# A list-scheduled attention and gating kernel: corrected operation times, new ranks, and fillers of the first gap counted at the lower clock

## Chip, cores, metric

One core of one Trainium2 chip. The metric is device time in microseconds of one execution, from runs without a profile; the profile comes from one more execution. The core has five engines with a queue of instructions each: TensorE (PE, matmuls into PSUM), VectorE (DVE), ScalarE (ACT), GpSimd (POOL) and SyncE (SP), which here issues all DMAs.

## What is computed

Attention over 4 batches, 8 heads, 768 positions and a head dimension of 64, with 8 global columns and a causal band of 96, then a gated layer with a spatial mixing step. Cut to what matters:

```
scores = q @ k.T / sqrt(D) - slope[h] * dist      # kept where global or within the band
a = softmax(scores);  x = a @ v                   # heads side by side: (4, 768, 512)
h = relu(x @ w_in);  u, v = halves of h
v_n = layernorm(v)
v_s = w_spatial @ v_n + b_spatial
out = (u * v_s) @ w_out
```

`w_in` and `w_out` arrive as float64.

## The kernel before

The work goes in 24 blocks of 128 positions, six to a batch. A block has scores (token S, four pairs of heads, two halves), the softmax, the transposes of the probabilities and their products with the values (token A), and behind it the gated layer of the batch in pieces: V and U (products with the two halves of `w_in`), G (spatial mixing) and O (product with `w_out`). From block 6 on each operand of a matmul is split into a high and a low part (names with `h` and `l` at the end) and three products are added up. The six blocks of batch 0 use plain fp32 matmuls, two passes each in the trace, because then the other engines are still setting up: bias tables, the pieces of `w_in` (token I, eight pieces of 128x512) and `w_out` (Q, eight of 128x256), rebuilt from float64 bits, and the spatial weights (T, six of 128x768).

A piece of weights is rebuilt in `split_weights`: ACT takes the absolute value of the upper words into a staging buffer (`raw` or `rawh`), a clamp between two limits follows (a tensor-scalar with max and min, on DVE or POOL as the planner chooses), then on DVE a shift-and-mask and two shift-ors with the words in `u` or `pth`, then a rounding into the high part (`w_in_h`, `w_out_h`) and a subtraction for the low part (`w_in_l`, `w_out_l`). For the spatial weights (`setup_w_t`) there is a rounding into `w_t_h` and a subtraction into `w_t_l`, which is always POOL's.

No order is written out by hand. A recorder collects all operations, with the engines that each may run on (`either`). `plan` simulates five engines: an operation becomes ready when those it depends on have ended by its estimate, each engine takes the ready operation with the lowest rank, and of several engines the one that would finish it first. An operation's rank is its token's number in the table `KEYS`. The estimates are in `cost`: nanoseconds as a constant plus a term in n, the elements of a row. Its third value says that the operation uses the port that DVE and POOL share; two such operations don't overlap in the plan. `keep_warm` then goes through the planned order and fills gaps of PE of over 0.9 us in the plan, up to 150 us, with fillers: transposes of the identity into a PSUM bank that is free. The first gap begins at `WARM_FROM`, 3000 ns. The operations are issued in the planned order; on the chip every engine keeps its order and waits on semaphores, whatever the real durations are.

All instructions of this path have line 39 in the profile, where the recorder calls the engine; they are told apart by their tiles. `pr` are probabilities, `mn` the minima that a score pass on DVE (CUSTOM_DVE_ANT_0, in the order ISA) also gives, `p`, `s`, `ops`, `m` PSUM banks for transposes, scores, attention outputs and the gated layer, `c` sums of attention outputs, `xth` and `xtl` their parts.

Of the kernel before, what the change touches and what calls it, by code (L numbers as in the profile page):

```python
# [194 lines left out]
def cost(op):  # L195

    out = op.writes[0]
    n = elements(out)
    src = op.reads[0] if op.reads else out
    psum = any(in_psum(x) for x in op.reads + op.writes[:1])  # L200
    parts = list(out.ap)[0][1]
    if op.eng == "tensor":
        if op.call == "transpose":
            return 109, 0, False
        n = elements(op.kw["rhs"])
        if op.kw["rhs"].dtype == F32:
# [78 lines left out]
def plan(ops, keys, trace=None):  # L285
# [145 lines left out]
WARM_FROM, WARM_GAP, WARM_TO = 3000.0, 900.0, 150000.0  # L431
# [3 lines left out]
def attn_then_spatial_gating_kernel(  # L435
# [712 lines left out]
```

## Time and profile before

| | |
|---|---|
| median of 3 runs | 483.08 us (482.77 to 485.05) |
| profiled execution, its own time | 483.04 us |
| its span, first to last instruction | 480.8 us |
| mean granted TensorE clock | 0.998 |
| busy: PE, DVE, ACT, POOL | 463.2, 351.8, 273.9, 267.1 us |

Busy times are of the 480.8 us. A matmul's end is modelled and overlaps the next, so PE's busy time is no measure of its work; distances from start to start are. A row gives a group of instructions with its engine, output, inputs, count, busy time, mean and the idle time before them, with what ended it ("<-").

### The profile page before, as it was taken

The numbers are of one execution on the slowest core, as the hardware profiler recorded it, in microseconds if no ns is written. First come the engines' busy times: TensorE is split into PE (matmuls) and PEld (weight loads), VectorE is DVE, ScalarE is ACT, GpSimd is POOL, SyncE is SP. The second block draws the span as 40 slices with busy tenths as digits, with TensorE's granted clock in tenths as the row PEclk, the third lists the DMA queues.
The fourth block names the chain that finished last, engine by engine and source line by source line (L and its number), as shares of the span: only waits on it lengthen the run. The fifth ranks groups of instructions, "written<-read, shape, count | busy, mean of one in ns | idle before, by whom it ended". The sixth has DMA issues, their size and how long they took to land.

```text
span 480.8 us, 9763 instructions
## 1 busy us (share of the span) xinstructions
PE 463.2 (96%) x3186; PEld 424.5 (88%) x3186; DVE 351.8 (73%) x1017; ACT 273.9 (57%) x764; POOL 267.1 (56%) x388
## 2 busy tenths in 40 slices
PE   7888999999999999999999999999999999999996
PEld 7666779999899999989998988999999989999995
DVE  4999998865788978878776687885679577653232
ACT  4855984544567777776354486774386366521111
POOL 4165675466756888798581456888268233551000
PEclk9999999999999999999999999999999999999999
DMA  7944512746578777657554727755386250000111
GB/s 226 328 133 139 183 49 74 199 121 164 135 190 218 193 190 192 169 156 180 149 141 123 201 84 197 188 152 125 73 219 171 65 144 35 0 1 3 44 45 50
DMA packets 35915, 65.47 MB, mean 136 GB/s; under 512 B 6065, under 2 KB 6321, under 8 KB 35857
## 3 DMA queue, kind: packets, MB, share of 16 engines
q1 hardware_dynamic: 35856, 64.77, 49.0%
q8 instruction: 27, 0.44, 0.4%
q14 instruction: 32, 0.25, 0.2%
HBM read 29.76 MB, written 6.68 MB: 76 GB/s over the span
## 4 chain that ended last, share of the span: by engine, by line
PE 77%; DVE 12%; DMA 4%; ACT 2%; SPq 2%; issue 1%; POOL 1%; DVEq 0%; ACTq 0%; POOLq 0%
PE m L39 55%; PE ops L39 8%; PE s L39 7%; PE p L39 7%; DVE raw L39 3%; DVE pr L39 2%; DVE c L39 2%; SPq L39 2%; DVE rawh L39 1%; DMA u<-in_moe_w_in_dram 1%; DMA vring<-in_moe_w_spatial_dram 1%; ACT pr L39 1%; DVE ev L39 1%; DVE w_in_l L39 1%; DMA kring<-raw 1%
## 5 line engine op out<-in xcount | busy, mean ns | idle before, releaser
L39 ACT ACTIVATE pr<-pr,mn 128x256 f32<-128x256 f32 (+1 forms) x192 | 92.0, 482 | 21.5 <-DVE mn L39 21.0
L39 DVE CUSTOM_DVE_ANT_0 pr<-s,bias 128x256 f32<-128x256 f32 (+1 forms) x192 | 68.3, 396 | 16.9 <-PE s L39 14.6
L39 DVE TENSOR_TENSOR c<-ops,c 64x256 f32<-64x256 f32 x168 | 70.6, 420 | 9.1 <-ACT c L39 4.4
L39 POOL TENSOR_SCALAR pr<-pr,rc 128x256 f32<-128x256 f32 (+1 forms) x144 | 66.9, 484 | 16.4 <-DVE rc L39 9.2
L39 PE MATMUL ops<-pth,vring 128*128 128x256 f32 x352 | 70.3, 313 | 2.5 <-ACT pth L39 1.8
L39 PE MATMUL s<-kring,q 128*128 128x256 f32 (+1 forms) x384 | 68.4, 303 | 3.3 <-DVE mn L39 2.1
L39 ACT ACTIVATE pth<-p 128x512 fp32r<-128x512 f32 (+3 forms) x96 | 52.3, 557 | 29.8 <-PE ops L39 15.3
L39 PEld LDWEIGHTS s<-kring,q 128*128 128x128 f32 x384 | 56.6, 189 | 9.0 <-DVE mn L39 3.7
L39 PEld LDWEIGHTS ops<-pth,vring 128*128 128x128 f32 x352 | 54.3, 189 | 8.1 <-ACT pth L39 3.1
L39 PE MATMUL p<-ident,pr 128*128 128x128 f32 x352 | 56.3, 273 | 1.7 <-ACT c L39 1.3
L39 DVE TENSOR_TENSOR pth<-p,pth 128x512 fp32r<-128x512 f32 (+1 forms) x72 | 45.4, 642 | 10.3 <-ACT pth L39 9.4
L39 PEld LDWEIGHTS p<-ident,pr 128*128 128x128 f32 x352 | 42.1, 140 | 8.1 <-ACT c L39 2.4
L39 PE MATMUL m<-w_t_h,vnh 128*128 128x256 f32 x288 | 44.8, 284 | 0.0
L39 PE MATMUL m<-w_t_h,vnl 128*128 128x256 f32 x288 | 44.7, 284 | 0.0
L39 PE MATMUL m<-w_t_l,vnh 128*128 128x256 f32 x288 | 43.1, 281 | 0.0
L39 DVE TENSOR_TENSOR ev<-m,b_bc 128x512 f32<-128x512 f32 x24 | 16.5, 688 | 36.3 <-PE m L39 36.3
L39 POOL TENSOR_TENSOR vnl<-ev,vnh 128x512 fp32r<-128x512 f32 x24 | 31.2, 1302 | 18.5 <-DVE vnh L39 9.3
L39 ACT ACTIVATE gh<-ev 128x512 fp32r<-128x512 f32 x24 | 15.1, 630 | 45.6 <-DVE ev L39 45.5
L39 ACT ACTIVATE ev<-m 128x512 f32<-128x512 f32 (+1 forms) x36 | 21.3, 591 | 34.0 <-PE m L39 33.3
L39 PEld LDWEIGHTS m<-w_t_h,vnh 128*128 128x128 f32 x288 | 38.5, 189 | 0.7 <-DVE ev L39 0.3
L39 PEld LDWEIGHTS m<-w_t_h,vnl 128*128 128x128 f32 x288 | 38.6, 189 | 0.2
L39 POOL TENSOR_TENSOR xtl<-c,xth 128x256 fp32r<-128x256 f32 x40 | 30.9, 773 | 13.9 <-ACT xth L39 13.7
(139 smaller groups left out, 1004.8 us busy)
## 6 DMA issues: line engine op xcount, KB each, us to landing
q<-rawh SPq DMA_DIRECT2D x72, 128.0 KB, 2.4
q<-raw SPq DMA_DIRECT2D x72, 128.0 KB, 2.4
out_dram<-ev SPq DMA_DIRECT2D x23, 256.0 KB, 2.8
raw<-in_q_dram SPq DMA_DIRECT2D x18, 256.0 KB, 3.0
raw<-in_v_dram SPq DMA_DIRECT2D x18, 256.0 KB, 2.9
raw<-in_k_dram SPq DMA_DIRECT2D x18, 256.0 KB, 3.3
kring<-rawh SPq DMA_DIRECT2D x36, 128.0 KB, 2.4
kring<-raw SPq DMA_DIRECT2D x36, 128.0 KB, 2.4
```

The costliest lines, as they stand in the source:

```text
L39: getattr(self.real, self.call)(*self.args, **self.kw)
```

## The change

Three edits. In `cost`, the estimates of some operations are replaced: among others POOL's clamps (until now 155 + 0.84 n) get 210 + 3.34 n, POOL's two-input operations and its products with a column get a little more, and several of DVE's and ACT's. In `keep_warm`, fillers of the first gap are counted with 185 ns each and no longer 112. And the table of ranks is another one: nearly all of its numbers are different.

```diff
         if in_psum(src):
-            return (175 + .85 * n, 0, False) if parts < P else (66 + .83 * n, 0, False)
+            return (175 + .85 * n, 0, False) if parts < P else (70 + .86 * n, 0, False)
         return 112 + .83 * n, 0, False
     if op.eng == "gpsimd":
         if n <= 8:
             t = 600 if op.kw.get("op") == ALU.pow else 280
         elif op.call == "tensor_tensor":
-            t = 148 + 2.17 * n
+            t = 148 + 2.21 * n
+        elif op.kw.get("op0") == ALU.max:
+            t = 210 + 3.34 * n
         elif isinstance(op.kw.get("scalar1"), bass.AP):
-            t = 244 + .82 * n
+            t = 270 + .9 * n
...
     if op.call == "reciprocal":
-        return 70 + 6.25 * n, 85, False
+        return 90 + 6.25 * n, 85, False
...
     if op.call in ("tensor_reduce", "bn_stats"):
-        return 70 + 1.04 * elements(src), 0, False
+        return 120 + 1.06 * elements(src), 0, False
     if op.call == "bn_aggr":
-        return 99, 0, False
-    return (190 if parts < P else 74) + 1.04 * n, 0, not one
+        return 145, 0, False
+    return (180 if parts < P else 66) + (1.04 if parts < P else 1.1) * n, 0, not one
...
                 if best and best[0] < last:
-                    out.extend(make(best[1]) for _ in range(int((gap - 300) // 112)))
+                    out.extend(make(best[1]) for _ in range(int((gap - 300) // (112 if last > WARM_FROM else 185))))
...
-KEYS = {'start': -11.92, ('P', 0): -8.84, ('bias', 0): -3.64, ('S', 0, 0): 19.47,
+KEYS = {'start': -18.36, ('P', 0): -14.95, ('bias', 0): 12.66, ('S', 0, 0): -4.23,
...
```

What it moves, at three places. First PE's and SP's beginning. PE's first rows are the fillers and the scores of block 0 (`kring` keys, `q` queries); of the difference:

```order
-L39 MATMUL s_103<-ident 128x128 x36
+L39 MATMUL s_103<-ident 128x128 x17
 L39 MATMUL s_103<-kring_97,q_0_95 128x128 x2
 L39 MATMUL s_106<-kring_97,q_0_95 128x128 x2
```

SP's first DMAs, before:

```order
L39 DMA vring_114<-in_v_dram 128x512
L39 DMA nraw<-in_n_global_dram 128x2
L39 DMA nraw<-in_n_local_dram 128x2
L39 DMA q_0_95<-in_q_dram 64x512 x2
L39 DMA kring_97<-in_k_dram 128x512
```

and now:

```order
L39 DMA nraw<-in_n_global_dram 128x2
L39 DMA nraw<-in_n_local_dram 128x2
L39 DMA q_0_95<-in_q_dram 64x512 x2
L39 DMA kring_97<-in_k_dram 128x512
L39 DMA q_0_96<-in_q_dram 64x512 x2
L39 DMA kring_97<-in_k_dram 128x512
L39 DMA u_119<-in_moe_w_in_dram 128x1024
L39 DMA vring_114<-in_moe_w_spatial_dram 128x768
L39 DMA kring_97<-in_k_dram 128x512
L39 DMA vring_114<-in_v_dram 128x512 x3
L39 DMA q_0_95<-in_q_dram 64x512 x2
L39 DMA u_115<-in_moe_w_in_dram 128x1024
```

There are 19 fillers fewer at the start, and the first load of values has gone from the head of SP's queue to behind the third block of keys. Further down PE gets fillers in four places (8, 5, 5 and 6) where two groups of 5 stood.

Second, POOL's queue behind the bias tables, before:

```order
L39 TENSOR_SCALAR kring_97<-kg 128x4x32
L39 TENSOR_SCALAR rawh_0_118<-rawh_0_118 128x512
L39 TENSOR_SCALAR xth_122<-c_1_129 128x2x128
L39 TENSOR_SCALAR w_t_h<-vring_114 128x768
L39 TENSOR_TENSOR w_t_l<-vring_114,w_t_h 128x768
L39 TENSOR_SCALAR xth_122<-c_2_134 128x2x128
L39 TENSOR_SCALAR kring_97<-kg 128x4x32
L39 TENSOR_TENSOR w_t_l<-vring_114,w_t_h 128x768
L39 TENSOR_TENSOR xtl_123<-c_2_134,xth_122 128x2x128
L39 TENSOR_SCALAR raw_113<-rc_102 128x512
L39 TENSOR_SCALAR rawh_0_121<-rawh_0_121 128x512
```

and now:

```order
L39 TENSOR_SCALAR w_t_h<-vring_114 128x768
L39 TENSOR_TENSOR w_t_l<-vring_114,w_t_h 128x768
L39 TENSOR_SCALAR kring_97<-kg 128x4x32
L39 TENSOR_SCALAR w_in_h<-raw_0_120 128x512
L39 TENSOR_SCALAR w_t_h<-vring_114 128x768
L39 TENSOR_TENSOR w_t_l<-vring_114,w_t_h 128x768
L39 TENSOR_SCALAR kring_97<-kg 128x4x32
L39 TENSOR_TENSOR xtl_123<-c_2_134,xth_122 128x2x128
L39 TENSOR_SCALAR w_t_h<-vring_114 128x768
L39 TENSOR_TENSOR w_t_l<-vring_114,w_t_h 128x768
L39 TENSOR_SCALAR raw_113<-rc_102 128x512
```

The clamps (`rawh` from `rawh`) are gone, here two of six in all, and the roundings into `xth`; roundings into `w_in_h` have come. Later two subtractions into `w_out_l` come too. DVE has the six clamps now.

Third, DVE where it rebuilds a piece of `w_in` (`raw` with `u`) and one of `w_out` (`raw` with `pth`), before:

```order
L39 SCALAR_TENSOR_TENSOR raw_0_120<-u_115,raw_0_120 128x512
L39 TENSOR_REDUCE rc_102<-sums_91 128x8
L39 SCALAR_TENSOR_TENSOR raw_0_116<-pth_125,raw_0_116 128x256
L39 SCALAR_TENSOR_TENSOR raw_0_120<-u_115,raw_0_120 128x512
L39 TENSOR_TENSOR c_1_129<-ops_93,c_0_128 64x256 x2
```

and now:

```order
L39 SCALAR_TENSOR_TENSOR raw_0_120<-u_115,raw_0_120 128x512
L39 SCALAR_TENSOR_TENSOR raw_0_116<-pth_125,raw_0_116 128x256
L39 TENSOR_TENSOR c_1_129<-ops_93,c_0_128 64x256 x2
L39 BN_STATS st_144<-ev_99 128x6
L39 COPY c_2_134<-p_126 128x256
L39 ISA pr_132,mn_101<-s_106,bias 128x256
L39 ISA mn_101 128x1
L39 TENSOR_TENSOR c_0_128<-ops_94,c_2_134 64x256 x2
L39 SCALAR_TENSOR_TENSOR raw_0_120<-u_115,raw_0_120 128x512
```

Between the two shift-ors of the same piece there were a reduction and another shift-or; now there are eight operations, six of which read PSUM.

## Rows read from the trace of the kernel before

**Rows 1.** Stages of the span: length, then each engine's busy us (count), clock, DMA.

```profile
0.00:12.00 12.00, 8.79 (x55) 8.60 (x55) 5.53 (x38) 4.97 (x19) 4.97 (x17) 1.00 0.71 226
12.00:72.00 60.00, 52.92 (x276) 42.15 (x274) 58.85 (x177) 46.47 (x143) 32.89 (x30) 1.00 0.51 167
72.00:476.00 404.00, 401.34 (x2860) 373.77 (x2858) 287.44 (x805) 222.04 (x604) 229.28 (x342) 1.00 0.49 129
476.00:480.80 4.80, 0.19 (x2) 0.00 (x0) 0.00 (x0) 0.39 (x1) 0.00 (x0) 0.84 0.36 121
```

**Rows 2.** Waits of PE after 76 us: who for whom, us in total, times, longest.

```profile
PE s L39 <- DVE mn L39: 0.7, 1, 0.7
PE ops L39 <- DVE pth L39: 0.6, 1, 0.6
PE m L39 <- ACT gh L39: 0.5, 1, 0.5
PE s L39 <- DMA kring<-raw: 0.5, 1, 0.5
PE p L39 <- DVE pth L39: 0.3, 1, 0.3
```

**Rows 3.** PE from 12 us: groups to 72 us, then two lines of time.

```profile
L39 PE MATMUL s<-kring,q 128*128 128x256 f32 x80 | 20.7, 387 | 2.0 <-DVE mn L39 1.2 <-issue 0.7
L39 PE MATMUL ops<-pth,vring 128*128 128x256 f32 x68 | 17.7, 385 | 1.8 <-ACT pth L39 1.8
L39 PE MATMUL p<-ident,pr 128*128 128x128 f32 x72 | 11.4, 276 | 1.5 <-ACT c L39 1.3 <-ACT pth L39 0.2
...
12.07 1.99 PE L39 MATMUL s<-kring,q 128*128 128x256 f32 x8
13.90 0.27 PE L39 MATMUL p<-ident,pr 128*128 128x128 f32 x1
```

**Rows 4.** The first 13 us in order of time: start, us, engine, what, idle before.

```profile
0.72 0.39 SPq L39 DMA_DIRECT2D vring<-in_v_dram  x1
...
1.17 0.42 SPq L39 DMA_DIRECT2D nraw<-in_n_global_dram  x1
...
3.05 6.65 PE L39 MATMUL s<-ident 128*128 128x128 f32 x36 [3.05 <-POOL ident masks.py:199]
...
7.10 0.37 POOL L39 TENSOR_SCALAR kg<-kring 128x128 f32<-128x128 f32 x1 [3.25 <-DMA kring<-in_k_dram]
...
7.98 0.17 DVE L39 COPY ev<-ev 128x32 f32<-128x32 f32 x1
...
9.54 1.06 PE L39 MATMUL s<-kring,q 128*128 128x128 f32 x8
10.19 0.29 DVE L39 CUSTOM_DVE_ANT_0 pr<-s,bias 128x128 f32<-128x128 f32 x1 [2.03 <-PE s L39]
```

**Rows 5.** Two stretches, columns as in rows 1.

```profile
3.05:8.20 5.15, 5.15 (x24) 5.15 (x25) 3.57 (x20) 1.58 (x8) 1.47 (x5) 1.00 0.72 217
...
12.00:24.00 12.00, 10.66 (x54) 7.73 (x52) 11.77 (x50) 10.79 (x39) 2.14 (x2) 1.00 0.97 328
```

**Rows 6.** Groups by form: POOL's clamps and w_t_l (17 to 70 us), DVE's clamps.

```profile
L39 POOL TENSOR_TENSOR w_t_l<-vring,w_t_h 128x768 fp32r<-128x768 f32 x6 | 11.4, 1903 | 4.8 <-ACT w_t_h L39 4.5
L39 POOL TENSOR_SCALAR rawh<-rawh 128x512 f32<-128x512 f32 x3 | 6.1, 2025 | 2.3 <-ACT rawh L39 2.1
...
L39 POOL TENSOR_SCALAR raw<-raw 128x256 f32<-128x256 f32 x2 | 2.1, 1064 | 4.7 <-ACT raw L39 4.7
...
L39 DVE TENSOR_SCALAR raw<-raw 128x512 f32<-128x512 f32 x4 | 1.6, 408 | 0.0
```

**Rows 7.** POOL and DVE side by side in order of time, columns as in rows 4.

```profile
24.28 0.66 POOL L39 TENSOR_SCALAR xth<-c 128x256 fp32r<-128x256 f32 x1
24.60 0.61 DVE L39 TENSOR_TENSOR xtl<-c,xth 128x256 fp32r<-128x256 f32 x1
25.98 2.13 POOL L39 TENSOR_TENSOR w_t_l<-vring,w_t_h 128x768 fp32r<-128x768 f32 x1
26.36 2.03 DVE L39 TENSOR_SCALAR rawh<-rawh 128x512 int32<-128x512 int32 x1
46.03 0.68 DVE L39 SCALAR_TENSOR_TENSOR raw<-u,raw 128x512 int32<-128x512 int32 x1
60.73 1.88 POOL L39 TENSOR_TENSOR w_t_l<-vring,w_t_h 128x768 fp32r<-128x768 f32 x1
60.84 2.31 DVE L39 SCALAR_TENSOR_TENSOR raw<-u,raw 128x512 int32<-128x512 int32 x1
```

More of the change, by code (lines that the diff above doesn't have):

```diff
@@ new lines @@
+KEYS = {'start': -18.36, ('P', 0): -14.95, ('bias', 0): 12.66, ('S', 0, 0): -4.23, ('S', 0, 1): 10.8, ('bias', 1): 28.65, ('W', 0): 2.33, (0, 'I', 1, 0): 3.19, (0, 'I', 1, 1): 12.55, (0, 'I', 1, 2): -8.76, (0, 'I', 1, 3): -12.58, ('P', 1): -10.38, ('A', 0, 0): 18.23, ('S', 1, 0): 13.95, ('A', 0, 1): 13.33, ('S', 1, 1): 0.63, ('W', 1): -3.3, (0, 'I', 0, 0): -7.89, (0, 'I', 0, 1): -82.57, (0, 'I', 0, 2): -11.69, (0, 'I', 0, 3): 6.16, (0, 'T', 0): -5.01, (0, 'T', 1): 55.84, ('P', 2): -3.53, ('A', 1, 0): 31.48, ('S', 2, 0): 42.4, ('A', 1, 1): -17.82, ('S', 2, 1): 21.11, ('W', 2): 1.8, (0, 'V', 0): 33.49, (0, 'V', 0, 1): 32.62, (0, 'B', 0): 11.45, (0, 'T', 2): -18.35, (0, 'T', 3): 20.37, ('P', 3): -5.38, ('A', 2, 0): 27.06, ('S', 3, 0): 24.81, ('A', 2, 1): 31.4, ('S', 3, 1): 11.96, ('W', 3): 28.25, (0, 'V', 1): 61, (0, 'V', 1, 1): 45.76, (0, 'U', 0, 0): 29.05, (0, 'U', 0, 1): -35.06, (0, 'T', 4): 31.15, (0, 'T', 5): 32.52, ('P', 4): 8.94, ('A', 3, 0): 27.18, ('S', 4, 0): 60.61, ('A', 3, 1): 31.11, ('S', 4, 1): 40.7, ('W', 4): 9, (0, 'V', 2): 29.04, (0, 'V', 2, 1): 41.53, (0, 'Q', 0, 0): 13.33, (0, 'Q', 0, 1): 19.75, (0, 'Q', 1, 0): 9.81, (0, 'Q', 1, 1): 12, ('P', 5): 10.38, ('A', 4, 0): 17.13, ('S', 5, 0): -12.33, ('A', 4, 1): 27.94, ('S', 5, 1): 46.7, ('W', 5): 68.99, (0, 'V', 3): 7.56, (0, 'V', 3, 1): 22.05, (0, 'U', 1, 0): 29.05, (0, 'U', 1, 1): 37.17, (0, 'Q', 2, 0): -4.71, (0, 'Q', 2, 1): -28.36, (0, 'Q', 3, 0): -22.55, (0, 'Q', 3, 1): 9.01, ('P', 6): 26.47, ('A', 5, 0): 20.95, ('S', 6, 0): -68.88, ('A', 5, 1): -21.27, ('S', 6, 1): -1.63, ('W', 6): -67.8, (0, 'V', 4): 18.21, (0, 'V', 4, 1): 31.37, (0, 'V', 5): 40.07, (0, 'V', 5, 1): -91.98, (0, 'U', 2, 0): 44.97, (0, 'U', 2, 1): -6.06, ('P', 7): 7.02, ('A', 6, 0): -8.59, ('S', 7): 9.65, ('A', 6, 1): 34.46, ('W', 7): -23.03, (0, 'G', 0, 0): 50.15, (0, 'G', 0, 1): 65.27, (0, 'O', 0, 0): -27.2, (0, 'O', 0, 1): 16.71, ('P', 8): -13.41, ('A', 7): 26.51, ('S', 8): 22.15, ('W', 8): 11.92, (0, 'G', 1, 0): 11.84, (0, 'G', 1, 1): 7.4, (0, 'O', 1, 0): 35.77, (0, 'O', 1, 1): 31.3, ('P', 9): 28.43, ('A', 8): 8.25, ('S', 9): 27.82, ('W', 9): 29.49, (0, 'G', 2, 0): 59.45, (0, 'G', 2, 1): 93.77, (0, 'O', 2, 0): 5.44, (0, 'O', 2, 1): 20.65, (1, 'V', 0): 10.6, (1, 'V', 1): 15.31, (1, 'U', 0): 46.22, ('P', 10): 18.59, ('A', 9): 20.23, ('S', 10): -8.68, ('W', 10): -24.71, (1, 'V', 2): 46.7, ('P', 11): -78.32, ('A', 10): 37.19, ('S', 11): 4.39, ('W', 11): -59.3, (1, 'V', 3): 10.2, (1, 'U', 1): 57.27, ('P', 12): 5.82, ('A', 11): 42.99, ('S', 12): 21.14, ('W', 12): 23.25, (1, 'V', 4): 12.38, (1, 'V', 5): -55.04, (1, 'U', 2): 77.71, ('P', 13): 45.36, ('A', 12): -15.44, ('S', 13): 8.5, ('W', 13): -14.31, (1, 'G', 0): 38.97, (1, 'O', 0): 35.69, ('P', 14): 63.88, ('A', 13): 85.33, ('S', 14): 8.15, ('W', 14): 15.86, (1, 'G', 1): -93.61, (1, 'O', 1): 21.46, ('P', 15): 5.89, ('A', 14): 19.7, ('S', 15): 16.37, ('W', 15): 47.65, (1, 'G', 2): 35.7, (1, 'O', 2): 32.39, (2, 'V', 0): 31.53, (2, 'V', 1): 45.53, (2, 'U', 0): -3.54, ('P', 16): 69.57, ('A', 15): 43.33, ('S', 16): -76.36, ('W', 16): 37.49, (2, 'V', 2): 77.24, ('P', 17): 4.91, ('A', 16): -8.36, ('S', 17): 17.6, ('W', 17): 43.71, (2, 'V', 3): 26.24, (2, 'U', 1): 56.65, ('P', 18): -2.95, ('A', 17): 28.34, ('S', 18): -5.47, ('W', 18): 67.08, (2, 'V', 4): 42.19, (2, 'V', 5): -6.19, (2, 'U', 2): 5.39, ('P', 19): 24.64, ('A', 18): 46.28, ('S', 19): 74.07, ('W', 19): 20.87, (2, 'G', 0): 2.61, (2, 'O', 0): 32.91, ('P', 20): 11.71, ('A', 19): 4.26, ('S', 20): 26.78, ('W', 20): 21.07, (2, 'G', 1): 26.19, (2, 'O', 1): 56.05, ('P', 21): 64.98, ('A', 20): 15.59, ('S', 21): -28.25, ('W', 21): 63.67, (2, 'G', 2): -0.86, (2, 'O', 2): 36.61, (3, 'V', 0): 13.18, (3, 'V', 1): 71.83, (3, 'U', 0): 85.9, ('P', 22): 12.74, ('A', 21): 32.45, ('S', 22): 43.3, ('W', 22): 55.18, (3, 'V', 2): 74.86, ('P', 23): -1.66, ('A', 22): 30.44, ('S', 23): 54.53, ('W', 23): 14.2, (3, 'V', 3): 23.7, (3, 'U', 1): 95.4, ('A', 23): 4.17, (3, 'V', 4): 6.87, (3, 'V', 5): 22.19, (3, 'U', 2): 23.05, (3, 'G', 0): -6, (3, 'O', 0): 54.91, (3, 'G', 1): 38.87, (3, 'O', 1): 46.21, (3, 'G', 2): 2.7, (3, 'O', 2): 68.06}
```

1 line of the change is left out of this document (removed).

## The prediction

> **What bounds the kernel now.** I read the stages first: four stretches of the span, and how full each engine is in them [rows 1]. From 72 us to 476 us TensorE (PE) is busy for 401 of 404 us, with 2860 instructions; nothing that other engines do there can shorten it by more than the waits it still has. Those I took from the waits of PE after 76 us: five of them, 2.6 us together, the two longest 0.7 and 0.6 us [rows 2]. So the place to look is before 72 us. There VectorE (DVE) is busy for 58.85 of 60 us [rows 1]: it computes the scores' minima, adds up the attention outputs, and rebuilds the double-precision weights, while PE issues only 276 instructions.
>
> Busy time of PE overlaps itself, so I price its work by start-to-start distances. An fp32 pass of 256 columns: eight start at 12.07 and the next instruction at 13.90, 0.229 us each [rows 3]. Between 12 and 72 us there are 80 + 68 such passes, 33.9 us; 72 transposes of probabilities at 0.11 us (below), 7.9 us; and the 56 others at the mean of the long stage, 404/2860 = 0.141 us, another 7.9 us [rows 1, 3]. That is 49.7 of 60 us: **some 10 us of gaps**. They, the time before the first real matmul (9.54 us) and the 4.8 us after PE's last work are what can change; the same matmuls remain in the program, and the tail's order is the old one.
>
> **The start.** PE begins with fillers, transposes of the identity that only keep it active. 36 start at 3.05 us and the first score matmul comes at 9.54 [rows 4]. 24 of them fill 3.05 to 8.20 [rows 5], 0.215 us each; the other 12 the remaining 1.34 us, 0.11 us each: the clock goes from its lower level (1.2 GHz) to 2.4 GHz about 8.2 us, and the fillers were counted as if it had been at 2.4 all along. Their data was ready earlier: POOL's copy out of the key block waited for that DMA and ran at 7.10; DVE finished the first bias at 8.15 (7.98 + 0.17) and then sat idle for 2.03 us until its first score pass at 10.19 [rows 4]. The change leaves 17 fillers: 17 x 0.215 = 3.7 us, over at 6.7 us. It also moves a load of values, which was first in SP's queue at 0.72 us, behind the keys and queries; the next issue stood at 1.17 [rows 4], so the lengths, queries and keys all come some 0.45 us sooner, the keys at 6.65, the bias at 7.7. Scores start at 6.7 us. At 2.4 GHz DVE's first pass followed the first matmul by 0.65 us (9.54 to 10.19); at half the clock I allow 1.3, which gives 8.0 in place of 10.19. Best -2.4 us (data limits, clock up at once), worst 0 (the lead is lost in the next wait); I take **-2.0**, near the best, because DVE is then full and its idle time is what goes.
>
> **The weight pieces and POOL.** Six of the 16 clamps of weight pieces ran on POOL, at 2.03 us (512 wide) and 1.06 us (256 wide); DVE does one of 512 in 0.41 [rows 6]. The planner thought them cheap (155 + 0.84 n ns); corrected, it sends all six to DVE. DVE gains 3 x 0.41 + 3 x 0.3 (estimated from the 512's) = 2.1 us, and gives up two of the weights' low-part subtractions, a rounding of weights, one of outputs and a broadcast copy, for an output copy and a narrower rounding: some 1.3 us net, by the same 0.41 us row. **+0.8 us** on the engine that bounds the stage, between 0 and 2.1.
>
> What the clamps did to the rest counts for more. When DVE and POOL both work on SBUF data, one waits. POOL's subtraction for the spatial weights (w_t_l, six times, 1.90 us) [rows 6] started at 25.98 and DVE's tensor-scalar beside it took 2.03 us; at 60.73 it started again and DVE's two-input shift-or took 2.31 us, against 0.68 for a clear one at 46.03 [rows 7]. That pattern occurs at five of the six, and costs DVE 1.0 to 1.6 us each time, about 8 us in all. DVE passes that read PSUM (scores, output sums) run beside it at their own length. The planner does know that the two exclude each other and puts PSUM work beside POOL's; but each clamp that runs 1.4 us over its estimate moves POOL's later operations away from their place. In the new order four of the six w_t_l are followed on DVE, in the plan's one list of all engines, by three or more operations with PSUM input or a reduction, and two by shift-ors after two passes or none. POOL also loses three roundings of outputs and gains three of weights and two subtractions: fewer operations beside DVE than before (nine go, five come). Not all of 8 us reached PE: it had about 10 us of gaps from every cause. I put 5.4 us of these to the collisions (about two thirds of 8), the range 0 to 5.4, and take half, **-2.7**, since two collisions are still in the plan and drift will make a third.
>
> Here a rule speaks against the change. A one-input POOL operation cost DVE too: POOL's rounding at 24.28 took 0.66 and DVE's subtraction beside it 0.61 [rows 7], some 0.2 over a clear 0.41. The Trainium skill (SBUF — State Buffer, Who interferes with whom) states that the shared port pair is an exclusive lock, that a DVE instruction with two SBUF inputs contends with any GpSimd one that reads SBUF, and that issue order decides who blocks. By it the five new POOL operations can each hold DVE for their full length, and the price would be the upper one of the slower rival below instead of nothing.
>
> **Fillers in later gaps.** 24 stand in the middle of the program where 10 stood. 14 x 0.11 = 1.5 us if PE would have had work, nothing if it waits, as it does for 10 us of this stage: **+0.4**, nearer to nothing.
>
> **After 72 us** operations move among DVE, ACT and POOL (ACT gains, POOL loses), engines with 71%, 55% and 57% of that stage [rows 1]; the waits there stay 2.6 us in my sum, 0 to 5 as bounds.
>
> Sum: -2.0 - 2.7 + 0.8 + 0.4 = -3.5 us. The profiled execution took 483.04 us (span 480.8), as good as the median of three, 483.08. Forecast **479.5 us**; its own range 477 to 481.5.
>
> **The rivals.**
> - *Almost all the gaps from collisions go, and half of the others:* -2.0 - 5.4 - 2.3 + 0.8 + 0.4 = -8.5, 474.5 us. For it: six mistimed clamps, each early in POOL's order, disturb everything behind them. Against it: two planned collisions, and the gaps that chains of dependent operations make.
> - *One of the two gains fails.* Without the collisions' part it is 483.0 - 2.0 + 1.2 = 482.2; without the start's 483.0 - 2.7 + 1.2 = 481.5. No measurable change. For it: weights and values share DMA engines that are 97% busy from 12 to 24 us [rows 5], and the second piece of weights now stands behind a spatial piece and values. One form of it is the clock: fillers end at 6.7 us, before the clock rose in the old run, and if it then rises only at 12 us, up to 3.8 us of matmuls from 8.2 us on take twice as long, which eats the start's 2.0. The Trainium skill (TensorE: Matmul & The Clock Gate, Part 4) says that transposes do not engage the full clock; by that the fillers had no part in it and the score matmuls alone must raise it. In this trace the spacing halved with nothing but fillers behind it, so the rule does not hold here, and I give this form 5 in 100.
> - *POOL blocks DVE more than before; slower.* If all six w_t_l meet a two-input DVE operation (6 x 1.6 = 9.6 us) and the five new POOL operations block for about 0.7 us each (3.5, from the 0.66 us row), DVE loses 13.1 us against some 9.5 now (the 8, and an estimated 1.5 for the shorter ones like the 0.2): +3.6, with DVE's +0.8, all fillers (+1.5) and a start that keeps only 1 us: about +4.9, 488 us; halfway there 485.5. With the other terms of the sum (-2.0 + 1.2) it decides from the point where DVE loses 3.2 us more than now. For it: the order was made by estimates, and a small drift brings any of these together. Against it: nine go, five come.
>
> **How the numbers follow.** 0.5% is 2.4 us, about what a measurement of this kernel can tell from no change; faster means under 480.7. Forecast case 0.44, of which 0.40 lies under that; first rival 0.16; no-change rival 0.26; slower rival 0.14. Faster 0.40 + 0.16 = 0.56; same 0.04 + 0.26 = 0.30; slower 0.14. The range takes in the first rival at its middle and half of the slower one: 474 to 485.
>
> **What would show it.** Right: the first score matmul near 7 us and DVE's idle before its first score pass under 0.5 us; no POOL clamp; at most three shift-ors or subtractions of over 1.2 us on DVE before 72 us; PE's 404 us of dense work begins about 3.5 us earlier, with unchanged length. Wrong: the start gained but the dense stage begins no earlier (collisions or DMA); spacing of 0.215 us beyond 10 us (clock); or PE's waits after 76 us over 5 us, which nothing in my sum foresees.

## The result, and the profile after

| | before | changed |
|---|---|---|
| median | 482.92 us (482.61 to 485.05, 4 runs) | 475.72 us (475.05 to 475.87, 4 runs) |
| ratio, 95% interval | | 0.9839 (0.9809 to 0.9869) |
| profiled execution, span | 483.04, 480.8 us | 475.74, 473.8 us |

The change is 7.2 us faster. I had forecast 3.5: the sign was right and the time lies in the range, but the size is twice the one I gave.

The stages of the changed kernel (stretch, length, busy us and count of PE, PEld, DVE, ACT and POOL, clock, DMA share, GB/s) answer to [rows 1]:

```profile
0.00:12.00 12.00, 8.84 (x45) 7.88 (x45) 7.66 (x54) 7.02 (x28) 4.96 (x17) 1.00 0.64 215
12.00:72.00 60.00, 56.25 (x316) 46.84 (x315) 56.75 (x175) 47.98 (x140) 28.55 (x30) 1.00 0.54 174
72.00:468.30 396.30, 395.43 (x2824) 369.57 (x2822) 280.21 (x791) 224.53 (x607) 220.61 (x331) 1.00 0.49 131
468.30:473.80 5.50, 0.22 (x2) 0.02 (x1) 0.00 (x0) 0.39 (x1) 0.00 (x0) 0.86 0.32 106
```

PE issues 316 instructions between 12 and 72 us where it issued 276 (14 of the 40 more are fillers), DVE is relieved a little, and PE's last matmul comes 7.7 us earlier. The first 10 us answer to [rows 4]:

```profile
0.72 0.39 SPq L39 DMA_DIRECT2D nraw<-in_n_global_dram  x1
...
3.05 3.89 PE L39 MATMUL s<-ident 128*128 128x128 f32 x17 [3.05 <-POOL ident masks.py:199]
...
7.59 0.17 DVE L39 COPY ev<-ev 128x32 f32<-128x32 f32 x1
8.10 0.29 DVE L39 CUSTOM_DVE_ANT_0 pr<-s,bias 128x128 f32<-128x128 f32 x1 [0.23 <-PE s L39]
```

The first score matmul begins at 6.87 us in place of 9.54, and DVE's idle time before its first pass is 0.23 us in place of 2.03. The waits of PE (who for whom, us in total, times, longest), the two longest of the first 76 us behind the fillers' start, and then from 76 us on, where they answer to [rows 2]:

```profile
PE m L39 <- DVE w_in_h L39: 1.8, 1, 1.8
PE s L39 <- DVE mn L39: 1.0, 1, 1.0
...
```

```profile
PE ops L39 <- DVE pth L39: 0.5, 1, 0.5
PE s L39 <- DMA kring<-rawh: 0.2, 1, 0.2
```

After 76 us 0.7 us are left of 2.6. The longest wait that remains is one meeting of DVE and POOL, in order of time:

```profile
26.37 1.85 POOL L39 TENSOR_TENSOR w_t_l<-vring,w_t_h 128x768 fp32r<-128x768 f32 x1
...
26.48 2.02 DVE L39 CAST w_in_h<-raw 128x512 fp32r<-128x512 f32 x1
...
28.56 0.50 PE L39 MATMUL m<-w_in_h,xth 128*128 128x512 f32 x1 [1.83 <-DVE w_in_h L39]
```

**Where 7.0 us of span went.** I took all distances between starts of PE's records, less the spacing that such an instruction has when nothing holds it (0.109 us for 128 columns, 0.119 for 256, 0.231 for 512, 0.216 for an fp32 pass), as pauses (work at a lower clock counts as a pause too):

| | before | changed | difference |
|---|---|---|---|
| first score matmul | 9.54 | 6.87 | -2.7 |
| pauses from there to 72 us | 12.45 | 8.46 | -4.0 |
| pauses after 72 us | 5.0 | 2.3 | -2.7 |
| fillers behind the start (14 more, 0.11 us each), missing records | | | +1.7 |
| from the start of PE's last matmul to the end | 4.87 | 5.59 | +0.7 |

How small a pause is counted moves the totals; the differences lie between -3.9 and -4.4 us up to 72 us and between -2.1 and -3.0 after it.

DVE's operations before 72 us ran 10.5 us over the length of a clear one of their kind (the 25th percentile of each) in the kernel before, nearly all of it beside POOL; now 5.4 us. Of POOL's six subtractions for the spatial weights (`w_t_l`) five held up a DVE operation before, by 1.0 to 1.6 us; now two do (a shift-or at 14.82 us that took 1.27 us for 0.69, and the rounding above). Beside the other four DVE does much work that reads PSUM, at its own length, as here:

```profile
46.85 2.28 POOL L39 TENSOR_TENSOR w_t_l<-vring,w_t_h 128x768 fp32r<-128x768 f32 x1 [1.17 <-ACT w_t_h L39]
47.45 0.86 DVE L39 TENSOR_TENSOR c<-ops,c 64x256 f32<-64x256 f32 x2
48.34 0.42 DVE L39 CUSTOM_DVE_ANT_0 pr<-s,bias 128x256 f32<-128x256 f32 x1
```

### The profile page after: what moved, and what is told of

Its sections match the earlier page's. It is cut to its first block, busy times and chain, and to the rows that moved or that the text cites. A ratio compares the mean times of both kernels' runs of the same rounds, so it can differ in the third digit from the quotient of the medians.

```text
span 473.8 us, 9730 instructions
## 1 busy us (share of the span) xinstructions
PE 460.7 (97%) x3181; PEld 424.3 (90%) x3181; DVE 344.6 (73%) x1016; ACT 279.9 (59%) x775; POOL 254.1 (54%) x378
## 4 chain that ended last, share of the span: by engine, by line
PE 87%; DVE 4%; SPq 3%; DMA 2%; ACT 2%; issue 1%; DVEq 0%
PE m L39 61%; PE ops L39 9%; PE s L39 9%; PE p L39 8%; SPq L39 3%; DMA vring<-in_v_dram 2%; DVE c L39 1%; ACT pr L39 1%; DVE raw L39 1%; DVE ev L39 0%; DMA kring<-rawh 0%; DVE pr L39 0%; DVE w_in_h L39 0%; DVE rawh L39 0%; DVE xtl L39 0%
## 5 line engine op out<-in xcount | busy, mean ns | idle before, releaser
L39 POOL TENSOR_SCALAR pr<-pr,rc 128x256 f32<-128x256 f32 (+1 forms) x144 | 68.1, 493 | 10.4 <-DVE rc L39 8.3
L39 PE MATMUL s<-kring,q 128*128 128x256 f32 (+1 forms) x384 | 69.8, 307 | 1.3 <-DVE mn L39 1.0
L39 PE MATMUL ops<-pth,vring 128*128 128x256 f32 x352 | 67.0, 311 | 0.7 <-DVE pth L39 0.5
L39 PEld LDWEIGHTS s<-kring,q 128*128 128x128 f32 x384 | 57.6, 191 | 7.1 <-DVE mn L39 2.4
L39 ACT ACTIVATE pth<-p 128x512 fp32r<-128x512 f32 (+3 forms) x96 | 52.3, 559 | 15.1 <-PE p L39 11.5
L39 PEld LDWEIGHTS ops<-pth,vring 128*128 128x128 f32 x352 | 53.1, 189 | 5.4 <-DVE pth L39 1.2
L39 PE MATMUL m<-w_t_h,vnl 128*128 128x256 f32 x288 | 43.7, 282 | 0.0
L39 POOL TENSOR_TENSOR xtl<-c,xth 128x256 fp32r<-128x256 f32 x40 | 29.8, 747 | 25.2 <-ACT xth L39 25.1
L39 ACT ACTIVATE c<-ops 64x256 f32<-64x256 f32 x72 | 27.3, 380 | 20.4 <-PE ops L39 17.9
```

The costliest lines, as they stand in the source:

```text
L39: getattr(self.real, self.call)(*self.args, **self.kw)
```

## The experiments

Ratios are to the kernel before, run on the same chip in turn; the changed kernel's is 0.9839 (0.9809 to 0.9869).

### The start alone, and undone

e1 is the kernel before with the new count of first fillers, e2 the changed kernel with the old one.

```diff
-  ... for _ in range(int((gap - 300) // 112)))
+  ... for _ in range(int((gap - 300) // (112 if last > WARM_FROM else 185))))
```

> The old order, with the change's count for the first gap alone: 22 fillers in place of 36, nothing else moved (the values' load stays first on SP). Theory 'the start is worth what it saves': 22 x 0.215 us end at 7.8 us, the first score matmul stands near 7.9 to 8.2 us (DVE's first bias is ready at 8.15) in place of 9.54, and the lead of about 1.5 us lasts to the end: 481.3 to 481.9 us. Rival 'the lead is lost in the next wait' (DVE's collisions with POOL come at the same places): the first score is as early, PE's gaps up to 72 us grow by as much, and the time is within 0.4 us of before. Rival 'clock': fewer fillers leave the spacing of PE's work at 0.215 us past 8.2 us, and the time is the same or longer.

> The new order, with the first gap's fillers counted as before: 28 in place of 17, all else the same. Theory 'the start is worth what it saves': 24 fillers at 0.215 us to 8.2 us and 4 at 0.11 end at 8.65 us, the first score comes 1.8 us later than in the new kernel, and the time is 1.4 to 1.9 us above its 475.7. Rival 'the lead is lost in the next wait': the gaps that follow shrink by as much, within 0.4 us of the new kernel.

e1: 481.60 us, ratio 0.9961 (0.9948 to 0.9974), 1.9 us shorter. e2: 476.72 us, 0.9859 (0.9842 to 0.9876), 1.0 us over the changed kernel, with intervals that overlap. The start of PE in e1, in order of time, and the largest group of PE's waits from 9 to 76 us in e2:

```profile
3.04 4.44 PE L39 MATMUL s<-ident 128*128 128x128 f32 x22 [3.04 <-POOL ident masks.py:199]
...
7.34 1.13 PE L39 MATMUL s<-kring,q 128*128 128x128 f32 x8
```

```profile
PE s L39 <- DVE mn L39: 2.8, 3, 2.2
...
```

In the old order the lead of 2.2 us lasts (1.9 of it in the time): DVE's idle time was what went. e1's waits after 76 us are those of [rows 2], each within 0.1 us of its size there, so they belong to the order and don't depend on when it begins. In e2 the first score is at 8.21 us, 1.34 later than in the changed kernel. Its trace is of the slowest of its six executions (479.30 us): it has one wait of 2.2 us for the minima of DVE's score pass, and then a granted clock of 0.51 from 18 to 21 us, so it says little about the start. e1 bears out the start's term in the old order; e2's 1.0 us doesn't settle it in the new one.

A single trace doesn't fix the lead either. In the four traces with the old order's start and 36 fillers (the kernel before, e5, e10, e17) the fillers' spacing halves at 8.2, 6.1, 8.9 and 7.1 us, and the first score comes at 9.54, 8.48, 9.86 and 9.01. In the six with the changed kernel's start and 17 fillers it comes between 6.76 and 7.57. Between the means lie 2.2 us; the 2.7 of the table above are a little more than is usual.

### Times or ranks

e3 has the new estimates in `cost` and the old ranks; e4 the new ranks and the old estimates. e9 and e10 add 1 ns to one estimate of the changed kernel and of the kernel before:

```diff
         elif op.call == "tensor_tensor":
-            t = 148 + 2.21 * n
+            t = 149 + 2.21 * n
```

and e11 takes back the clamps' estimate alone:

```diff
-        elif op.kw.get("op0") == ALU.max:
-            t = 210 + 3.34 * n
```

> The old ranks and the old count of fillers, with the corrected times of operations alone: the planner makes a new order out of them. Theory 'the times did it' (a plan with true times puts POOL's and DVE's operations beside work that they do not block, in every stage): without the start's 2.7 us it comes within 1.5 us of the new kernel plus 2.7, so 477 to 480 us; no clamp on POOL, PE's gaps up to 72 us near the new kernel's 8.5 us and after 72 us near its 2.3 us. Rival 'the ranks did it' (ranks are tuned to one set of times, and another set makes an untuned order of them): 482 us or more, with gaps up to 72 us at 11 us or more though no clamp is on POOL. In between, 480 to 482 us: both.

> The new ranks and the new count of fillers, with the old times of operations: the other half of the change. Theory 'the times did it': the start's lead stays, and the rest falls back to the old gaps or worse, 480 us or more, with clamps on POOL again. Rival 'the ranks did it': within 1.5 us of the new kernel, 474.5 to 477.2 us. What the start alone would leave is 483 - 2.7 = 480.3 us, so a time above that says that the ranks without their times lose.

> The new kernel with one time of its table longer by 1 ns: POOL's two-input operations at 149 + 2.21 n in place of 148, as near to the measured 1.85 us of the 768-column one (1.846) as the table itself (1.845). The planner, asked again with the same ranks, gives another order from PE's 22nd row on. Theory 'truth of the times gives the gain': within 1 us of the new kernel. Rival 'ranks and times are one matched pair, and any other order of this planner is an untuned one': 480 us or more, with PE's gaps after 72 us well over the new kernel's 2.3 us.

> The kernel before with the same 1 ns added to its own time of POOL's two-input operations (149 + 2.17 n). The order changes from PE's 106th row on. Theory 'matched pair': it is slower than before by 2 us or more, with more gaps behind the place where the order changes. Rival 'truth of the times': the times are as good or bad as they were, so within 1 us of before.

> The new kernel with the clamp's price alone put back to the old one (155 + 0.84 n, for a measured 2.03 us): some clamps go to POOL again, and everything is planned anew. Theory 'the clamp's price is the correction that matters, by what it does on POOL': like the run with six clamps put on POOL in place, 476.5 to 479 us. Rival 'matched pair': 485 us or more, with the loss spread over PE's waits after 72 us, where no clamp is near.

| | time | ratio | PE's pauses after 72 us |
|---|---|---|---|
| e3 | 503.49 us | 1.0429 (1.0410 to 1.0448) | 19.6 us, and 80 more fillers than before |
| e4 | 521.48 us | 1.0802 (1.0769 to 1.0835) | 48.3 us |
| e9 | 510.67 us | 1.0590 (1.0565 to 1.0615) | 30.0 us, and 53 more fillers than in the changed kernel |
| e10 | 490.10 us | 1.0153 (1.0134 to 1.0171) | 12.5 us |
| e11 | 512.65 us | 1.0624 (1.0602 to 1.0645) | 26.1 us, and 76 more fillers than in the changed kernel |

Each half of the change alone makes the kernel slower by 20 or 38 us, and one nanosecond in one estimate costs the changed kernel 35 us, the clamps' estimate alone 37. The waits are spread over every chain. The longest groups of PE's waits after 76 us in e4, and then in e9:

```profile
PE m L39 <- ACT xth L39: 13.0, 7, 3.9
PE ops L39 <- DVE pth L39: 3.1, 5, 2.1
```

```profile
PE m L39 <- ACT xth L39: 4.3, 2, 2.4
PE p L39 <- POOL pr L39: 3.5, 1, 3.5
```

So neither "the times did it" nor "the ranks did it" holds: the table of ranks gives its order under its own estimates only, and under the other sets tried, a truer one included, it gives another order and a worse one. I take it that the ranks were searched for one set of estimates; no run shows how they were found. In e10 the order is the old one up to PE's 106th row, and its pauses to 72 us are as before (12.2 us); its loss begins at 348 us, with 7.3 us of pauses between 348 and 384. A price in such a planner can't be judged by changing it alone.

### The clamps in place

e5 takes the old plan, e6 the new one, and only the engine of six clamps is set after planning (to DVE in e5, to POOL in e6); the order in the one list stays. The edit of e5:

```diff
+        planned = plan(nc.ops, KEYS)
+        clamps = [op for op in nc.ops if op.call == "tensor_scalar" and op.kw.get("op0") == ALU.max and op.kw.get("op1") == ALU.min]
+        for op in clamps:
+            if op.eng == "gpsimd":
+                op.take(0)
```

> The old order of every engine as it stands, with the six clamps of POOL done by DVE at the same place in the plan's one list; nothing is planned anew. Theory 'the mispriced clamps threw POOL's later work out of its place': with them gone from POOL its later operations stand where the planner wanted them, collisions of DVE up to 72 us fall from 10.5 us to 7 or less, PE's gaps there from 12.5 us to under 11 in spite of 2.1 us more work on DVE, and the time falls by 1 to 3 us. Rival 'the clamps did no harm in place': DVE does 2.1 us more in the stage that it bounds, collisions stay at 9 to 11 us at other places, and the time is the same to 2 us longer.

> The new order as it stands, with six clamps of weight pieces given back to POOL at the same place in the list. Theory 'the mispriced clamps threw POOL's later work out of its place': POOL's later operations slip by 0.7 to 1.6 us behind each, PE's gaps up to 72 us grow from 8.5 us to 10 or more, and the time is 2 to 5 us above the new kernel's 475.7. Rival 'the clamps did no harm in place': DVE is relieved of 2.1 us and the time is the same or up to 1 us shorter.

e5: 482.55 us, 0.9986 (0.9973 to 1.0000). e6: 477.08 us, 0.9878 (0.9843 to 0.9912), 1.4 us over the changed kernel as medians stand, with overlapping intervals. In e5 DVE still loses 10.1 us to meetings with POOL. Two of them, in order of time:

```profile
23.73 2.06 POOL L39 TENSOR_TENSOR w_t_l<-vring,w_t_h 128x768 fp32r<-128x768 f32 x1
24.05 2.03 DVE L39 TENSOR_TENSOR xtl<-c,xth 128x256 fp32r<-128x256 f32 x1
...
43.44 1.86 POOL L39 TENSOR_TENSOR w_t_l<-vring,w_t_h 128x768 fp32r<-128x768 f32 x1
43.55 2.29 DVE L39 SCALAR_TENSOR_TENSOR rawh<-u,rawh 128x512 int32<-128x512 int32 x1
```

The old order's meetings come without any clamp on POOL: they come with that order, and not from what the mispriced clamps pushed aside, as I had it (though e5 gives DVE 2.1 us more to do, so not all stands where the planner put it). The clamps may cost something on POOL in the new order, by medians a fifth of the gain, but the intervals don't tell it from nothing, and e6's trace (478.67 us) has a granted clock of 0.55 from 15 to 18 us, which the changed kernel's trace doesn't have.

### The fillers behind the start

```diff
-WARM_FROM, WARM_GAP, WARM_TO = 3000.0, 900.0, 150000.0
+WARM_FROM, WARM_GAP, WARM_TO = 3000.0, 900.0, 9000.0
```

> The new kernel without the 24 fillers behind the start; nothing else moves. Theory 'they cost PE time': in its trace work follows some of them at once, 0.11 us each, so the time falls by 0.4 us (only where PE had no wait behind them) to 2.6 us (all of them). Rival 'clock': without them PE's longest pauses up to 35 us lower the granted clock and the spacing of its transposes goes to 0.215 us for a time: 1 us or more above 475.7. Rival 'they stand in waits anyway': PE's gaps grow by what the fillers took, and the time is within 0.4 us.

475.33 us, 0.9837 (0.9814 to 0.9859): no difference. What the 24 fillers took (2.6 us) came back as pauses, 13.0 us in all for 10.8. Part of these are waits that the fillers had stood in, and part is the clock. Two stretches of e7 and then the same of the changed kernel (columns as in the stages):

```profile
15.00:18.00 3.00, 2.13 (x9) 1.48 (x8) 2.42 (x6) 2.59 (x12) 1.72 (x3) 0.68 1.03 363
18.00:24.00 6.00, 5.99 (x28) 4.87 (x28) 4.17 (x15) 3.72 (x12) 0.00 (x0) 0.87 1.04 331
```

```profile
15.00:18.00 3.00, 2.71 (x18) 1.87 (x17) 2.55 (x6) 2.78 (x12) 1.86 (x3) 1.00 1.02 334
18.00:24.00 6.00, 6.00 (x32) 5.01 (x31) 4.96 (x17) 3.92 (x12) 0.00 (x0) 1.00 1.04 313
```

PE of e7 there, in order of time:

```profile
14.12 1.13 PE L39 MATMUL s<-kring,q 128*128 128x256 f32 x4 [1.18 <-DVE mn L39]
16.07 0.69 PE L39 MATMUL p<-ident,raw 128*128 128x128 f32 x2 [0.82 <-ACT pth L39]
...
17.72 1.91 PE L39 MATMUL ops<-pth,vring 128*128 128x256 f32 x4
19.43 1.93 PE L39 MATMUL s<-kring,q 128*128 128x256 f32 x8
21.19 1.03 PE L39 MATMUL ops<-pth,vring 128*128 128x256 f32 x4
```

After waits of 1.18 and 0.82 us four fp32 passes took from 17.72 to 19.43, 0.43 us each, twice the 0.22 of the eight that follow: PE was at 1.2 GHz and then at 2.4 again. So the fillers pay for themselves here: nothing gained, nothing lost.

That the fillers keep the clock up is shown only in part. Two of the other traces that have them show the low clock at the same place, behind one longer wait (2.23 us in e2, 1.57 us in e6). First e2, then e6:

```profile
18.00:21.00 3.00, 2.95 (x13) 2.38 (x12) 1.04 (x5) 2.25 (x9) 0.62 (x1) 0.51 1.04 364
```

```profile
15.00:18.00 3.00, 3.00 (x11) 2.58 (x12) 2.52 (x6) 2.56 (x11) 2.36 (x3) 0.55 0.98 293
```

And two of e7's five executions have a mean clock of 0.999 over the whole span, as high as with the fillers.

### Single meetings of DVE and POOL

e8 gives the rounding of 26.48 us to ACT; e12 gives the two subtractions that met DVE at 13.7 and 26.4 us to DVE; e18 is e12 with e7's edit. The edit of e12:

```diff
+        planned = plan(nc.ops, KEYS)
+        low = [op for op in planned if op.eng == "gpsimd" and op.call == "tensor_tensor" and op.writes[0].shape[-1] == 768]
+        for x in (0, 1):
+            low[x].ways = ((nc.vector, "tensor_tensor", (), low[x].kw),)
+            low[x].take(0)
```

> The new kernel with one operation moved: the rounding of a weight piece that DVE did at 26.48 us beside POOL's subtraction (2.02 us, and PE waited 1.83 us for it) is done by ACT, which is idle from 27.0 to 30.1 us. Theory 'the collision holds up PE there': ACT has the piece ready at 27.6 us, PE's wait of 1.83 falls to about 0.9, and the time is 0.7 to 1.5 us shorter. Rival 'DVE loses the 2 us all the same': its next operation beside POOL's subtraction takes the 2 us instead, the low part and the next score minimum come no earlier than 0.4 us before, PE waits for them at the next place, and the time is within 0.4 us of the new kernel.

> The new order with two of POOL's six subtractions for the spatial weights, those that met DVE at 13.7 and 26.4 us, done by DVE at the planned place. I estimate 0.9 to 1.0 us each on DVE (768 columns, against 0.68 us for its subtraction of 512), for 0.9 + 1.6 us of collisions that go. Theory 'the two collisions hold up PE': PE's gaps at 12.9 and 26.3 us (1.2 and 2.0) fall to under 1 us together, and the time is 0.7 to 2 us shorter than the new kernel's 475.7. Rival 'DVE is full, the loss only moves': within 0.5 us of it.

> The new kernel with both edits that left it no slower: two of POOL's subtractions on DVE, and no fillers behind the start. Theory 'the two add up': with the collisions gone PE has work behind some of the fillers, so their removal is worth more here than alone: 473.5 to 474.8 us. Rival 'the fillers stand in waits still': 474.5 to 475.5 us, no shorter than with the two subtractions alone.

e8: 475.75 us, 0.9845 (0.9825 to 0.9866). e12: 474.93 us, 0.9841 (0.9823 to 0.9860). e18: 474.99 us, 0.9833 (0.9811 to 0.9855). None is measurably shorter than the changed kernel, and e18 takes as long as e12, so the two edits don't add up. e8 in order of time:

```profile
11.51 0.83 POOL L39 TENSOR_SCALAR w_t_h<-vring 128x768 fp32r<-128x768 f32 x1 [2.12 <-DMA vring<-in_moe_w_spatial_dram]
...
12.43 1.81 POOL L39 TENSOR_TENSOR w_t_l<-vring,w_t_h 128x768 fp32r<-128x768 f32 x1
12.66 1.85 DVE L39 TENSOR_SCALAR raw<-raw 128x512 f32<-128x512 f32 x1
...
15.37 0.91 PE L39 MATMUL s<-kring,q 128*128 128x256 f32 x3 [1.96 <-DVE mn L39]
...
28.41 0.51 PE L39 MATMUL m<-w_in_h,xth 128*128 128x512 f32 x1 [0.89 <-ACT w_in_h L39]
```

The wait for `w_in_h` fell from 1.83 to 0.89 us. That isn't the moved rounding's doing alone: POOL's second subtraction came 2.2 us earlier than in the changed kernel, and met DVE's shift-or in place of the rounding, which cost DVE 1.0 us there:

```profile
24.21 1.87 POOL L39 TENSOR_TENSOR w_t_l<-vring,w_t_h 128x768 fp32r<-128x768 f32 x1
24.90 1.73 DVE L39 SCALAR_TENSOR_TENSOR raw<-u,raw 128x512 int32<-128x512 int32 x1
```

And POOL's first pair began at 11.51 us, because its load landed 1.2 us earlier than in the changed kernel's trace (12.71), met another operation of DVE, and PE waited 1.96 us there for 1.0. On DVE the moved subtraction takes 0.95 us and the two meetings are gone (e12's pauses to 72 us: 6.7 us for 8.5, in the fastest of its five executions, 473.30 us), yet the time falls by 0.8 us as medians stand, which the intervals don't resolve. In this stage the meetings are partly a matter of when a load lands.

### The waits after 72 us

The kernel before has two meetings of DVE and POOL where two of its later waits are. In order of time:

```profile
122.13 1.30 POOL L39 TENSOR_TENSOR gl<-ev,gh 128x512 fp32r<-128x512 f32 x1 [4.47 <-ACT gh L39]
122.26 1.72 DVE L39 TENSOR_TENSOR raw<-raw,rawh 128x512 fp32r<-128x512 f32 x1
...
124.71 0.50 PE L39 MATMUL s<-kring,q 128*128 128x256 f32 x2 [0.73 <-DVE mn L39]
...
233.12 2.51 DVE L39 TENSOR_TENSOR ev<-ev,u 128x512 f32<-128x512 f32 x1
233.81 1.28 POOL L39 TENSOR_TENSOR raw<-raw,rawh 128x512 fp32r<-128x512 f32 x1
...
236.35 0.74 PE L39 MATMUL m<-w_out_h,gh 128*128 128x512 f32 x2 [0.54 <-ACT gh L39]
```

e17 puts one operation of each pair on the other engine, all else as before:

```diff
+        low, gl, late = nc.ops[1192], nc.ops[1161], nc.ops[2748]
+        low.take(1)
+        planned.remove(low)
+        planned.insert(planned.index(gl) + 1, low)
+        late.ways = ((nc.vector, "tensor_tensor", (), late.kw),)
+        late.take(0)
```

> The kernel before with two operations on other engines, both after 72 us: DVE's subtraction of 122.26 us (1.72 us beside POOL's gl) goes to POOL behind gl, and POOL's subtraction of 233.81 us (beside which DVE's ev<-ev,u took 2.51 us) goes to DVE behind ev. Theory 'PE's waits there come from the same meetings of DVE and POOL': DVE's two long operations are gone, PE's pauses at 123.6 and 235.5 us (0.9 and 0.7 us) fall to 0.3 or less, and the time falls by 1.0 to 1.6 us. Rival 'another chain ends last there' (the transfers that wait for the moved operations, or a later pause that grows): the two pauses move or stay, and the time is within 0.5 us of before.

481.34 us, 0.9969 (0.9956 to 0.9983), 1.5 us shorter by the ratio and 1.3 by the medians. The waits of PE after 76 us in e17:

```profile
PE s L39 <- DMA kring<-raw: 0.8, 1, 0.8
PE ops L39 <- DVE pth L39: 0.6, 1, 0.6
PE s L39 <- issue: 0.4, 1, 0.4
PE p L39 <- DVE pth L39: 0.3, 1, 0.3
```

The waits for `mn` and `gh` are gone; the one for `kring` grew by 0.3. So about half of the 2.7 us that the changed kernel gained after 72 us was to be had in the old order, from two meetings of the kind that I had counted before 72 us alone. Where the other half comes from wasn't tried.

### Are plans kept?

The planner's own begin of PE's last matmul can be set beside the trace's. These are the numbers that the kernel's `plan` computes, no measurements. For e13 to e16 I searched other ranks: random changes of the table, kept where they made this begin earlier (and at times where not, so as not to stick). e13 and e14 use the corrected estimates, e15 and e16 the old ones; all four have the new count of first fillers.

```diff
-KEYS = {'start': -18.36, ('P', 0): -14.95, ('bias', 0): 12.66, ('S', 0, 0): -4.23,
+KEYS = {'start': -2019.69, ('P', 0): -1671.32, ('bias', 0): 242.42, ('S', 0, 0): 264.25,
...
```

> The new kernel with other ranks: found from the old ones by random changes that were kept where the kernel's own planner, with the corrected times, let PE's last matmul begin earlier. By the planner that is 476.1 us here (its own reckoning, no measurement; 466.7 in the new kernel, where the trace shows 468.2 and the run takes 475.7, 9.0 more than the plan; 465.0 in the kernel before, where the trace shows 475.9 and the run takes 482.9, 17.9 more). Theory 'kept plan': PE's last matmul begins within 3 us of the plan, and the time is 485 us, 483 to 488. Rival 'luck': the trace leaves the plan by 8 us or more, as in the kernel before, 492 us or more.

> As e13, with a second search: planned begin of PE's last matmul 475.0 us. Theory 'kept plan': 484 us, 482 to 487. Rival 'luck': 491 us or more.

> The kernel before (with the new count of the first fillers) and other ranks, found by the same search under the old times: planned begin of PE's last matmul 471.0 us, earlier than in e13 and e14. Theory 'kept plan': under the old times the plan is not kept; PE's last matmul begins 6 to 10 us after the plan, the time is 486.7 us (484 to 490), no shorter than e13 and e14 though it was planned 4 to 5 us shorter. Rival 'luck' (or: the errors of the old times do not matter): 9 us over the plan, 480 us.

> As e15, with a second search: planned begin of PE's last matmul 474.4 us, about that of e14. Theory 'kept plan': 490 us (487 to 493), 4 to 8 us above e14. Rival 'luck' (or no effect of the times): 483.4 us, within 2 us of e14.

The times were 484.37 us (1.0029, 1.0015 to 1.0043), 488.72 (1.0131, 1.0110 to 1.0151), 482.81 (1.0011, 0.9998 to 1.0024) and 495.48 (1.0251, 1.0213 to 1.0290). PE's last matmul, plan and trace; the trace's row of the changed kernel gives the first of two, and the second begins 0.12 us later:

```profile
468.12 0.40 PE L39 MATMUL s<-w_out_h,gl 128*128 128x256 f32 x2
```

| corrected estimates | plan | trace | | old estimates | plan | trace | |
|---|---|---|---|---|---|---|---|
| changed kernel | 466.7 | 468.2 | +1.5 | before | 465.0 | 475.9 | +10.9 |
| e9 | 504.5 | 503.2 | -1.3 | e10 | 473.8 | 483.5 | +9.7 |
| e3 | 495.1 | 495.3 | +0.2 | e4 | 513.3 | 515.0 | +1.7 |
| e13 | 476.1 | 477.0 | +0.9 | e15 | 471.0 | 474.5 | +3.5 |
| e14 | 475.0 | 482.2 | +7.2 | e16 | 474.4 | 489.4 | +15.0 |

Under the corrected estimates four plans of five are kept to 1.7 us, under the old ones one of five. Part of the old ones' 10.9 and 9.7 us is the start, whose fillers the plan doesn't count: e1, with fewer of them, begins PE's last matmul at 473.8, 8.8 over the same plan. e11, where the clamps' estimate alone is wrong, is planned at 499.6 and begins at 505.5, 5.9 over. e13 came out as "kept plan" said; e14 was 5 us over it, and has 9.2 us of meetings before 72 us where e13 has 5.5; e16 was worse than both theories had it, and e15 lies between them. So the theory holds for the table as a whole, not for each order: with corrected estimates more of the orders ran as planned, four of five against one, which is few to call it a rule. The changed kernel was even planned 1.7 us later than the kernel before, and runs 7.7 us earlier. Why the one order in five breaks its plan under corrected times isn't settled. The clock alone isn't it: e14's trace is granted 0.50 from 29 to 32.4 and from 49.5 to 52.9 us, which by estimate (half of 6.8 us) can have cost up to 3.4 of its 7.2 us, but e13's is granted 0.50 from 40 to 46.7 us and its plan is kept. Most of the loss in e3 and e9 is in the plan already: the planner's order, and not the chip, has the gaps.

## Why the size was wrong

- **The start** (-2.0; measured -2.7 in the first score, -2.1 in DVE's first pass, 1.9 in the time of e1) was right, and so was its step that DVE's idle time goes. The rival with the late clock didn't come: in the changed kernel the scores' starts are 0.21 us apart up to 7.9 us and 0.11 from 8.1 us on; in the kernel before the fillers' spacing halved at 8.2 us. (The clock column can't show this: it reads 1.00 also from 3.05 to 8.20 us in [rows 5], where the spacing was 0.215 us.) The rule of the Trainium skill that I had set against it (TensorE: Matmul & The Clock Gate, Part 4), that transposes don't engage the full clock, doesn't hold in these traces: in e1 the fillers' spacing goes from 0.21 to 0.11 us at 6.8 us, before any other matmul (the first score is at 7.34).
- **After 72 us** is the step that failed: "the waits there stay 2.6 us in my sum". They fell to 0.7 us in the waits' view, and the pauses fell by 2.7 us, which is most of what my sum lacked. I had kept 0 to 5 as bounds, and had asked of that stage only which engines are full (71% and less), not what ended each wait. Two of the five were DVE held by POOL in a stage where both have time to spare: an engine that is 71% busy can still be the last one for a single matmul. e17 shows these two to be worth 1.5 us; the rest of the 2.7 stays open.
- **The collisions** (-2.7 and +0.8 for the clamps on DVE, +0.4 for fillers, -1.5 together): PE's pauses fell by 4.0, of which the 14 more fillers only took the place of 1.5, so the stage gave some -2.5, 1.0 more than forecast. The fillers cost nothing measurable (e7), and the +0.8 doesn't show. "Half" was right as a count, 10.5 us to 5.4, and so was the step that the new order puts DVE's work on PSUM beside POOL's subtractions: I had expected three meetings of six, there are two. That the fewer meetings made the pauses shorter is argued from these counts; no run takes the meetings before 72 us out of the old order, and e12, which takes two more out of the new one, gains nothing measurable. One reason behind the term was wrong: clamps on POOL that run 1.4 us over their estimate don't explain the old meetings, which stay when they are taken away (e5).
- **The tail** (0): +0.7 us, from the start of PE's last matmul to the end. It is within what one order shows from trace to trace: 4.75 to 5.54 us in the kernel before, e1, e5, e10 and e17, 4.83 to 5.59 in the changed kernel, e7, e8, e12 and e18.
- **The rivals.** The time came near the first rival's 474.5 us, but not by its way: it put all of its gain before 72 us, 7.7 us of gaps, where the pauses fell by 4.0. The slower rival didn't come: DVE's loss to POOL fell by 5.1 us and didn't grow.
- What I said would show it came: no clamp on POOL, first score near 7 us, DVE's idle time 0.23 us, one shift-or or subtraction of over 1.2 us on DVE before 72 us where there were five. Only one sign told of the error: the dense work began about 5 us earlier and not 3.5, and its length shrank.

My sum treated the change as edits whose prices add up. The runs say that the unit is the whole order, ranks and estimates together: either of them with another partner was slower in all five runs that tried it (e3, e4, e9, e10, e11).

## What to carry to other kernels

In a kernel whose order comes from a planner with searched priorities, estimates and priorities are one piece: change an estimate and search again, or leave both, and never judge one of them alone. Corrected estimates seem worth having because the plan was then mostly kept on the chip (four orders of five here), so that a search is rewarded; set the plan's end beside the trace's to see whether it is. And look at each remaining wait of the bound engine for what ended it, in stages where nothing is full as well: there a single pair of operations that exclude each other was worth some 0.7 us (1.5 us for the two in e17).

## What the runs showed of the hardware

- POOL's load of spatial weights landed at 11.5 to 12.7 us in kernels with the same order of DMAs (e8, the changed kernel), while the 16 DMA engines were full (share 1.01 in e8 from 9 us to the landing, 1.03 in the changed kernel); whom POOL then met on DVE changed with it.
- Behind a wait of 3.5 us without fillers the clock was low. In e9 PE stood still until 195.58 us; of the two stretches, the second is granted 0.57:

```profile
192.00:196.00 4.00, 0.48 (x3) 0.20 (x2) 2.98 (x16) 3.65 (x14) 4.00 (x7) 1.00 0.79 191
196.00:200.00 4.00, 3.83 (x13) 2.72 (x13) 2.43 (x5) 1.50 (x3) 3.92 (x9) 0.57 0.86 206
```

  The mean clock of e9 is 0.988 and of e4 0.978, against 0.998: an order with long waits pays for them twice.
- DVE's subtraction of 768 columns with both operands in SBUF takes 0.95 us (e12's two, 954 ns each) and POOL's 1.82 to 2.28 (the changed kernel's six); the longest meetings cost DVE 1.6 us. To leave such an operation to POOL "because it has time" costs DVE more than doing it, when they meet for that long.
